# A table of due-time offsets for a planned attention and MLP kernel, replaced by another

## The chip, the cores and the metric

The kernel runs on one core of a Trainium2 chip. The metric is the device time of one execution in microseconds. Before the change it is 624.45 us, the median of three runs (622.62, 624.45 and 626.06). One further execution was taken with the hardware profiler: 630.24 us, of which 628.4 us are the span of the profile. TensorE does the matrix products, VectorE (DVE), ScalarE (ACT) and GpSimd (POOL) work on rows, and SyncE (SP) issues the transfers.

## The reference

The inputs are q, k and v of shape (4, 8, 1152, 64): 4 batches of 8 heads, 1152 positions, 64 numbers each; a weight of 512 x 1024, one of 1024 x 512 and a vector of 1024.

```python
q_pool = q.reshape(B, H, S // 2, 2, D).mean(axis=3)
scores = scale * np.matmul(q_pool, k.transpose(0, 1, 3, 2))
scores = scores - np.max(scores, axis=-1, keepdims=True)
attn = np.exp(scores)
attn = attn / (np.sum(attn, axis=-1, keepdims=True) + 1e-09)
x = np.matmul(attn, v)           # then heads side by side: 2304 rows of 512
h = x @ w_in
e = np.exp(h - np.max(h, axis=-1, keepdims=True))
solu = h * (e / (np.sum(e, axis=-1, keepdims=True) + 1e-09))
mu, var = np.mean(solu, -1, keepdims=True), solu.var(-1, keepdims=True)
ln = (solu - mu) / np.sqrt(var + 1e-06) * g_ln
out = ln @ w_out
```

So there are 32 heads of 576 queries against 1152 keys, and behind them 2304 tokens that go through two weight matrices.

## The kernel before

**Attention.** The heads are taken as 16 pairs. For a pair, keys and pooled queries are loaded, scaled and split into a coarse part and a remainder in 16 bits: the largest value qm of the queries (L683), a scale qs from it (L691, L698 and the reciprocal L703), the coarse queries qa (ACT, L823), their remainder qb (VectorE, by the helper at L473), the coarse keys (GpSimd, L722, for pair 1) and the remainder kn of the keys (VectorE, L473 again). SyncE turns qa, qb and kn by DMA transposes (L837, L733) and copies pieces on: khi (L738), w2h (L1102) and zq (L843), which holds the last 64 queries of both heads of a pair. zq reads the turned qa.

For each head TensorE first makes scores whose row maxima VectorE takes (L982, L977, L988). They are turned, shifted (L994), and put into a row of the query operand by a DMA (L1003, L1005); in the first pairs another way is used (L1011, L1021). Then TensorE makes the scores proper, a key tile of 128 at a time; ACT takes the exponential once in 32 and once in 16 bits (L1133, L1139), GpSimd forms the remainder (L1160), and TensorE multiplies with the values (vhi, vlo, from L911 and L918). VectorE divides by the sums and writes x (L1242).

**Tokens.** Each batch gives four token tiles of 128 and one half tile; SyncE merges two half tiles into one (xm, L1563). A tile is normalized, turned (xt, L1345), multiplied with w_in, goes through the exponential (L1384) and the layer norm (L1459), is turned again (lt, L1464), multiplied with w_out, copied and stored (L1539). The weights are themselves prepared from raw loads (L535) with the casts at L544 and VectorE's L554 and L560.

**What sets the order.** No step stands in the code in the order in which it runs. Each is registered with an engine, a length, a due time and what it reads and writes, and a planner orders all of them: at any moment of its own reckoning an engine takes the ready step with the smallest due time for which there is a buffer. The due time is a formula of the kernel's constants KP (L23) plus an offset from the table OFF (L24), which is looked up by the group of the step: the name of the first tile that it writes and the number of its pair, head or tile, as `kn.1` or `zq.9`.

```python
at += OFF.get(self.group((writes or reads)[0]), 0)
```

Due times also decide who gets a buffer or a bank first. After the planning each engine runs its steps in a fixed order, and waits on semaphores for what others make.

Of the kernel before, what the change touches and what calls it, by code (L numbers as in the profile page):

```python
# [42 lines left out]
class Plan:  # L43
# [50 lines left out]
    def add(self, engine, length, at, fn, reads=(), writes=(), mark=None, kind="round", also=(), calls=1, port=0):  # L94
        at += OFF.get(self.group((writes or reads)[0]), 0)
        o = Op(n=len(self.ops), engine=engine, length=length, at=at, fn=fn, mark=mark, kind=kind, calls=calls)
        o.port = port or engine == "POOL"
        reads, writes, also = ([self.place(k) for k in x] for x in (reads, writes, also))
        deps = o.deps
        for k in self._keys(reads):  # L100
            if k in self.writers:
                deps[self.writers[k]] = True
        for k in writes:
            if k in self.writers:
                deps[self.writers[k]] = True
            for r in self.readers[k]:
                deps.setdefault(r, False)
        deps.pop(o, None)
        for k in self._keys(reads):
            self.readers[k].append(o)  # L110
        for k in writes:
            self.writers[k] = o
            self.readers[k] = []
            self.parts[k[:2]][k] = 1
        for k in (*reads, *writes, *also):
            b = k[:2]
            if (b[0] in self.tags or b[0] in self.banks) and b not in o.uses:
                if b not in self.users:
                    o.new.append(b)
                o.uses.append(b)  # L120
                self.users[b] += 1
        self.ops.append(o)
# [1548 lines left out]
```

## Time and profile before

| what | value |
| --- | --- |
| median of three runs | 624.45 us |
| profiled execution | 630.24 us |
| its span | 628.4 us |
| TensorE busy | 594.5 us (95%) |
| VectorE busy | 505.1 us (80%) |
| ACT busy | 506.7 us (81%) |
| GpSimd busy | 469.0 us (75%) |
| mean granted TensorE clock | 0.98 |

The busy time counts what an engine executes, not its waits. The granted clock is the share of TensorE's full speed, 2.4 GHz, that it was given; 0.50 is 1.2 GHz, and a number between is a stretch of which a part was at either level. The chain that ended last is followed back from the last instruction, at each step to what released it; where TensorE has 71% of it, the rest is time in which TensorE waited for somebody.

### The profile page before, as it was taken

The numbers are of one execution on the slowest core, as the hardware profiler recorded it, in microseconds if no ns is written. First come the engines' busy times: TensorE is split into PE (matmuls) and PEld (weight loads), VectorE is DVE, ScalarE is ACT, GpSimd is POOL, SyncE is SP. The second block draws the span as 40 slices with busy tenths as digits, with TensorE's granted clock in tenths as the row PEclk, the third lists the DMA queues.
The fourth block names the chain that finished last, engine by engine and source line by source line (L and its number), as shares of the span: only waits on it lengthen the run. The fifth ranks groups of instructions, "written<-read, shape, count | busy, mean of one in ns | idle before, by whom it ended". The sixth has DMA issues, their size and how long they took to land.

```text
span 628.4 us, 17256 instructions
## 1 busy us (share of the span) xinstructions
PE 594.5 (95%) x6630; PEld 368.2 (59%) x6635; DVE 505.1 (80%) x1189; ACT 506.7 (81%) x978; POOL 469.0 (75%) x491
## 2 busy tenths in 40 slices
PE   8978989998888899999999999999999999999997
PEld 6747666765545465565665556556566666654453
DVE  6966788989799998878977999888989887529460
ACT  5866787998889889888998798898989989946361
POOL 5796666665777889898899889788999989932130
PEclk9996979999899899999999999999999999999999
DMA  9183967387987658767748679767697453146322
GB/s 262 35 177 98 205 179 165 75 189 154 187 225 149 133 103 182 150 151 128 142 76 144 158 142 189 139 148 111 129 164 133 81 103 79 29 67 117 69 50 68
DMA packets 183790, 83.00 MB, mean 132 GB/s; under 512 B 168604, under 2 KB 169372, under 8 KB 183708
## 3 DMA queue, kind: packets, MB, share of 16 engines
q1 hardware_dynamic: 183196, 81.18, 63.5%
q8 instruction: 52, 0.85, 0.6%
q10 hardware_dynamic: 512, 0.72, 0.3%
q14 instruction: 30, 0.25, 0.1%
HBM read 36.70 MB, written 4.72 MB: 66 GB/s over the span
## 4 chain that ended last, share of the span: by engine, by line
PE 71%; DVE 16%; ACT 4%; POOL 2%; DMA 2%; issue 2%; SPq 1%; DVEq 0%; POOLq 0%; ACTq 0%
PE bank L463 68%; DVE mx L982 6%; POOL eh L1160 2%; PE bank L1639 1%; ACT e L1139 1%; DMA zq<-q 1%; DVE wb L473 1%; DVE kn L473 1%; DVE eh L1153 1%; DVE mx L977 1%; ACT eh L1139 1%; DMA q<-c 1%; DVE ln L1459 1%; PE bank L743 1%; DVE wb L554 1%
## 5 line engine op out<-in xcount | busy, mean ns | idle before, releaser
L1160 POOL TENSOR_TENSOR eh<-e,eh 128x512 f16<-128x512 f32 (+1 forms) x278 | 331.7, 1212 | 65.2 <-ACT e L1139 24.0
L982 DVE TENSOR_REDUCE mx<-bank 128x1 f32<-128x512 f32 (+1 forms) x300 | 188.0, 653 | 25.5 <-PE bank L463 24.5
L463 PEld LDWEIGHTS <-eh 128*128 128x128 f16 x3246 | 137.9, 99 | 66.0 <-issue 9.5
L1139 ACT ACTIVATE e<-bank 128x512 f32<-128x512 f32 (+1 forms) x259 | 154.0, 614 | 24.6 <-POOL eh L1160 11.6
L1139 ACT ACTIVATE eh<-bank 128x512 f16<-128x512 f32 (+3 forms) x257 | 151.6, 616 | 27.5 <-PE bank L463 26.1
L463 PE MATMUL bank<-vhi,eh 128*128 128x65 f16 x2159 | 149.8, 196 | 7.1 <-DVE x L1242 3.0
L463 PE MATMUL bank<-q,w 128*128 128x64 f16 (+2 forms) x612 | 142.5, 294 | 6.1 <-ACT e L1139 2.2
L463 PE MATMUL bank<-q,w2h 65*128 65x512 f16 (+1 forms) x540 | 127.3, 288 | 0.0
L463 PE MATMUL bank<-w,q 128*128 128x512 f16 (+2 forms) x390 | 109.1, 339 | 4.2 <-DVE mx L982 2.6
L463 PE MATMUL bank<-wb,xt 128*128 128x512 f16 x432 | 113.0, 379 | 0.0
L463 PE MATMUL bank<-wb,lt 128*128 128x512 f16 x432 | 110.5, 379 | 0.1
L463 PE MATMUL bank<-vlo,eh 128*128 128x64 f16 x1087 | 104.5, 195 | 0.0
L463 PEld LDWEIGHTS <-w2h 65*128 65x128 f16 x540 | 45.2, 98 | 32.4 <-issue 9.3
L463 PEld LDWEIGHTS <-w 128*128 128x128 f16 x540 | 46.6, 98 | 23.9 <-issue 2.2
L463 PEld LDWEIGHTS <-lt 128*128 128x128 f16 x432 | 38.8, 98 | 37.0 <-issue 0.4
L463 PEld LDWEIGHTS <-xt 128*128 128x128 f16 x432 | 38.0, 98 | 36.5 <-issue 2.6
L1166 POOL TENSOR_TENSOR er<-r,er 128x320 f16<-128x320 f32 (+1 forms) x60 | 51.3, 857 | 8.7 <-ACT er L1150 5.0
L463 PEld LDWEIGHTS <-q 128*128 128x128 f16 x360 | 31.3, 99 | 21.1 <-issue 3.6
L1360 DVE TENSOR_REDUCE st<-bank 128x1 f32<-128x512 f32 x36 | 24.3, 682 | 21.3 <-PE bank L463 21.3
L1384 ACT ACTIVATE e<-bank,st,xs 128x512 f32<-128x512 f32 x36 | 27.7, 777 | 14.9 <-DVE st L1363 9.8
L1422 POOL TENSOR_TENSOR st<-st 128x1 f32<-128x1 f32 x18 | 4.3, 239 | 38.4 <-DVE st L1411 36.8
L1150 ACT ACTIVATE r<-bank 128x320 f32<-128x320 f32 (+1 forms) x60 | 25.6, 431 | 4.0 <-PE bank L463 3.8
(143 smaller groups left out, 900.8 us busy)
## 6 DMA issues: line engine op xcount, KB each, us to landing
vx<-in_v_dram SPq DMA_DIRECT2D x32, 288.0 KB
kt<-in_k_dram SPq DMA_DIRECT2D x31, 288.0 KB
qt<-in_q_dram SPq DMA_DIRECT2D x15, 576.0 KB
out_dram<-o SPq DMA_DIRECT2D x35, 128.0 KB
khi<-w SPq DMA_DIRECT2D x30, 144.0 KB
w2h<-w SPq DMA_DIRECT2D x30, 144.0 KB
raw<-in_moe_w_in_dram SPq DMA_DIRECT2D x8, 511.6 KB
raw<-in_moe_w_out_dram SPq DMA_DIRECT2D x8, 511.6 KB
```

What stands on the lines that cost most here:

```text
L463: nc.tensor.matmul(out=o, lhsT=a, rhs=b, start=first, stop=last, skip_group_check=True)
L473: eng.scalar_tensor_tensor(out=o, in0=a, scalar=scale, in1=b, op0=ALU.mult, op1=ALU.subtract)
L554: nc.vector.scalar_tensor_tensor(out=w32.bitcast(I32), in0=tl["raw", n][:, :, 0], scalar=5, in1=tl["wps", n].bitcast(I32), op0=ALU.logical ...
L743: nc.tensor.transpose(ps[:, c, :], tl["kt", 0][:, h, 3 * i + c, :], ident)
L977: nc.vector.tensor_reduce(out=tl["mx", g][:, 0:4, 2], in_=tl["nps", (g, m, c)], op=ALU.max, axis=AXX)
L982: nc.vector.tensor_reduce(out=tl["mx", g][:, m, c:c + 1], in_=tl["nps", (g, m, c)], op=ALU.max, axis=AXX)
L1139: nc.scalar.activation(out=o if P else o.rearrange("p (f i) -> p f i", f=2), in_=i, func=ACTF.Exp, scale=esc)
L1150: nc.scalar.activation(out=o, in_=tl[rn(u), (g, u)], func=ACTF.Exp, scale=esc)
L1160: eng.tensor_tensor(out=e[:, o:o + c.stop - c.start], in0=e32[:, c], in1=e[:, c], op=ALU.subtract)
L1166: eng.tensor_tensor(out=e[:, :, 1, :], in0=tl["r32", (g, u)][:, 0:len(RU[u]), :], in1=e[:, :, 0, :], op=ALU.subtract)
L1360: nc.vector.tensor_reduce(out=st(f), in_=tl[H_[f]], op=ALU.max, axis=AXX)
L1384: nc.scalar.activation(out=tl[E][:, f * 512:(f + 1) * 512], in_=tl[H_[f]], func=ACTF.Exp, bias=st(2), scale=xs[:, r, 3:4], accum_out=st(3 ...
```

## The change

The table OFF at L24 is replaced. Before it had 1049 entries, now it has 1058; 1042 groups are in both, and 4 of these have the same value. Nothing else in the code differs: not KP, not the planner, not a length or a buffer. The number of instructions of each kind on each engine is the same, and the steps of each engine are the same steps. In the order of 1872 planned TensorE steps, 1258 can be left where they are while the others are moved around them; on VectorE 829 of 1126, on SyncE 277 of 369.

```diff
-OFF = {'am.0': 28.38, 'am.1': -49.32, 'am.10': 1.42, 'am.11': -2.84, ...
+OFF = {'am.0': -39.66, 'am.1': -70.36, 'am.10': -7.68, 'am.11': -4.98, ...
```

The first place is on VectorE, where pair 1's keys and queries are made ready while the maxima of head 1 are taken: qm is the largest query, qs the scale, qb and kn the remainders, mx the maxima. Before:

```order
L683 TENSOR_REDUCE qm<-qt 128x1
L982 TENSOR_REDUCE mx<-bank 128x1 x2
L691 TENSOR_REDUCE qs<-bank 128x1
L698 TENSOR_SCALAR qs<-qs 128x1 x2
L982 TENSOR_REDUCE mx<-bank 128x1
L703 RECIPROCAL qs<-qs 128x1
L982 TENSOR_REDUCE mx<-bank 128x1
L1011 TENSOR_REDUCE mz<-mx 128x3
L982 TENSOR_REDUCE mx<-bank 128x1 x3
L473 SCALAR_TENSOR_TENSOR qb_85<-qt,qs,qa 128x9x64
L1021 TENSOR_SCALAR q_160<-bank 1x384
L473 SCALAR_TENSOR_TENSOR kn<-kt,qs,kn 128x18x64
```

The same place after the change:

```order
L683 TENSOR_REDUCE qm<-qt 128x1
L982 TENSOR_REDUCE mx<-bank 128x1 x2
L691 TENSOR_REDUCE qs<-bank 128x1
L698 TENSOR_SCALAR qs<-qs 128x1 x2
L982 TENSOR_REDUCE mx<-bank 128x1
L703 RECIPROCAL qs<-qs 128x1
L982 TENSOR_REDUCE mx<-bank 128x1 x2
L1011 TENSOR_REDUCE mz<-mx 128x3
L473 SCALAR_TENSOR_TENSOR qb_85<-qt,qs,qa 128x9x64
L1021 TENSOR_SCALAR q_161<-bank 1x384
L473 SCALAR_TENSOR_TENSOR kn<-kt,qs,kn 128x18x64
```

Between the reciprocal and qb stand two maxima instead of four; ahead of L683 one fewer is left too, and behind kn follow five instead of two.

The second place is on GpSimd, a little earlier: vlo is the remainder of the first pair's values, qt the pooled queries of pair 1, the COPY of L752 fills the operand w2 of head 1, and L1160 is the remainder of the exponentials. Before:

```order
L755 MEMSET w_193 1x1152
L918 TENSOR_TENSOR vlo<-vx_80,vhi_82 128x1152
L679 TENSOR_TENSOR qt<-qt 128x576
L521 MEMSET zq_86 128x128
L1160 TENSOR_TENSOR eh<-e_323,eh 128x64
```

After:

```order
L755 MEMSET w_194 1x1152
L752 COPY w_194<-w_180 64x384 x3
L918 TENSOR_TENSOR vlo<-vx_80,vhi_82 128x1152
L521 MEMSET zq_86 128x128
L679 TENSOR_TENSOR qt<-qt 128x576
```

The three copies, which stood between remainders of the exponentials some twenty rows further down, now come ahead of vlo; on ACT, L911, which vlo waits for, and the statistics L871 of the next pair have changed places.

The third place is on SyncE, where pair 9 is turned and copied on: w2h, khi and zq are operands of the score products, xm is the merged half tile, out_dram the output. Before:

```order
L651 DMA qt<-in_q_dram 128x1152
L837 DMA_TRANSPOSE q_5020<-qb_85 128x9x64 x2
L1102 DMA w2h_79<-w_4478 64x1152
L837 DMA_TRANSPOSE q_5081<-qa 128x9x64 x2
L733 DMA_TRANSPOSE w_5139<-kn 128x9x128
L843 DMA zq_86<-q_5081 64x64 x2
L1563 DMA xm<-x 64x512
L738 DMA khi<-w_5139 64x1152
```

After:

```order
L651 DMA qt<-in_q_dram 128x1152
L837 DMA_TRANSPOSE q_5027<-qb_85 128x9x64 x2
L733 DMA_TRANSPOSE w_5073<-kn 128x9x128
L837 DMA_TRANSPOSE q_5107<-qa 128x9x64 x2
L1102 DMA w2h_79<-w_4493 64x1152
L738 DMA khi<-w_5073 64x1152
L1563 DMA xm<-x 64x512
L843 DMA zq_86<-q_5107 64x64 x2
```

The copies into zq, which stood ahead of the merge xm, now stand behind it.

## Rows read from the trace of the kernel before

**Rows 1.** Head of the page: span, busy time by engine, granted clock, chain by engine

```profile
span 628.4 us, 17256 instructions
...
PE 594.5 (95%) x6630; PEld 368.2 (59%) x6635; DVE 505.1 (80%) x1189; ACT 506.7 (81%) x978; POOL 469.0 (75%) x491
...
PE 71%; DVE 16%; ACT 4%; POOL 2%; DMA 2%; issue 2%; SPq 1%; DVEq 0%; POOLq 0%; ACTq 0%
```

**Rows 2.** Busy by stretch: window, PE, PEld, DVE, ACT, POOL; PEclk, DMA share, GB/s

```profile
0.00:260.00 260.00, 234.00 (x2598) 157.92 (x2604) 220.28 (x492) 214.56 (x415) 190.57 (x200) 0.95 0.70 158
260.00:624.00 364.00, 360.48 (x4034) 210.31 (x4032) 284.78 (x699) 291.43 (x564) 278.47 (x292) 1.00 0.61 115
40.00:60.00 20.00, 15.91 (x116) 12.08 (x115) 13.66 (x29) 12.13 (x21) 14.08 (x21) 0.75 0.54 143
80.00:100.00 20.00, 18.01 (x207) 13.36 (x207) 15.37 (x36) 13.71 (x26) 9.55 (x8) 0.83 0.60 160
...
200.00:220.00 20.00, 17.14 (x158) 8.65 (x158) 19.08 (x46) 18.13 (x35) 17.05 (x18) 0.91 0.61 136
```

**Rows 3.** The same by stretches of 3 us, ahead of and behind the clock's falls

```profile
45.00:48.00 3.00, 1.66 (x18) 1.29 (x17) 2.39 (x7) 2.62 (x5) 3.00 (x4) 1.00 1.01 261
...
51.00:54.00 3.00, 3.00 (x25) 2.75 (x23) 1.67 (x4) 1.91 (x4) 1.42 (x2) 0.50 0.06 20
...
84.00:87.00 3.00, 1.44 (x6) 0.48 (x5) 2.97 (x8) 2.55 (x4) 2.75 (x3) 1.00 0.87 254
```

**Rows 4.** Timeline, TensorE: start, us, instruction, count, [idle before <- releaser]

```profile
39.62 0.59 PE L463 MATMUL bank<-w,q 128*128 128x512 f16 x2
...
49.00 0.32 PE L463 MATMUL bank<-khi,zq 128*128 128x384 f16 x1 [2.34 <-DMA zq<-q]
...
58.87 1.04 PE L463 MATMUL bank<-w,q 128*128 128x512 f16 x2
```

**Rows 5.** TensorE's waits, grouped: us in total, times, longest

```profile
PE bank L463 <- DMA zq<-q: 3.6, 2, 2.3
```

**Rows 6.** Timeline, SyncE's queue, pair 1

```profile
29.88 2.64 SPq L837 DMA_TRANSPOSE q<-qb  x2
...
42.09 1.24 SPq L843 DMA_DIRECT2D zq<-q  x2
```

**Rows 7.** Timeline, VectorE, pair 1

```profile
26.73 1.53 DVE L982 TENSOR_REDUCE mx<-bank 128x1 f32<-128x384 f32 x3
28.18 1.64 DVE L473 SCALAR_TENSOR_TENSOR qb<-qt,qs,qa 128x576 f16<-128x576 f32 x1
...
30.44 1.42 DVE L473 SCALAR_TENSOR_TENSOR kn<-kt,qs,kn 128x1152 f16<-128x1152 f32 x1
```

**Rows 8.** Timeline, GpSimd, from 19 to 43 us

```profile
19.28 2.39 POOL L918 TENSOR_TENSOR vlo<-vx,vhi 128x1152 f16<-128x1152 f32 x1 [9.02 <-ACT vhi L911]
21.63 1.42 POOL L679 TENSOR_TENSOR qt<-qt 128x576 f32<-128x576 f32 x1
...
26.24 3.21 POOL L722 TENSOR_SCALAR kn<-kt,qs 128x1152 f16<-128x1152 f32 x1
...
41.22 1.40 POOL L752 CAST w<-w 64x384 fp32r<-64x384 f32 x3
```

**Rows 9.** Timeline, the queue, VectorE and TensorE near 300 us, pair 9

```profile
298.65 1.17 SPq L843 DMA_DIRECT2D zq<-q  x2
300.54 0.46 SPq L1563 DMA_DIRECT2D xm<-x  x1
...
300.02 0.49 DVE L1242 TENSOR_TENSOR x<-bank,r 128x320 f32<-128x320 f32 x1
...
309.11 0.32 PE L463 MATMUL bank<-khi,zq 128*128 128x384 f16 x1
```

**Rows 10.** Timeline, TensorE, the last matmuls

```profile
610.28 13.54 PE L463 MATMUL bank<-wb,lt 128*128 128x512 f16 x62
```

2 lines of the change are left out of this document (1 added, 1 removed).

## The prediction

> **What bounds the kernel now.** First the head of the profile's page [rows 1]. TensorE is busy for 594.5 of 628.4 us, and 71% of the chain that ended last is its own work. So the time can only fall by the 33.9 us in which TensorE idles, and by what it loses at the lower of its two clock levels. Next the view by stretches [rows 2]: 26.0 of the 33.9 idle microseconds lie before 260 us (260.00 − 234.00), 3.5 between 260 and 624, and the rest (4.4) behind the last matmul. Behind 260 us the granted clock is 1.00 throughout, so only the first 260 us have anything to give, while anything behind them can be lost.
>
> The clock: in the stretches 40:60 and 80:100 the mean granted clock is 0.75 and 0.83 [rows 2], which is 10.0 us and 6.8 us at 1.2 GHz instead of 2.4 (twice the shortfall from 1, times 20 us). At 51:54 it reads 0.50 right behind a stretch, 45:48, in which TensorE was busy for 1.66 of 3 us; 84:87, with 1.44 of 3 us, stands ahead of the second fall [rows 3]. What half clock costs: two matmuls of 512 columns take 1.04 us at 58.87 and took 0.59 at 39.62 [rows 4], so 43% of a time at half clock is lost where TensorE has no other wait: 4.3 of the 10.0 us, 2.9 of the 6.8.
>
> The longest wait of TensorE for one result is the one at 49.00: 2.34 us for the DMA that writes zq [rows 4], 2.3 of the 3.6 us that this DMA costs in all [rows 5]. Followed back: zq is written by SyncE's queue (issues from 42.09); that queue begins pair 1 with the transposes of qb at 29.88 [rows 6], and works without a gap from there to zq; qb is written by VectorE at 28.18 for 1.64 us [rows 7], so it ends at 29.82, 0.06 us before the queue starts.
>
> **The change part by part.** Only the table OFF differs, numbers that are added to the due time of each group of steps. The set of instructions is the same on every engine; their order is not. A time in it acts only through order, so I asked of each stretch with a wait what now stands ahead of the step that is waited for.
>
> *Pair 1's keys and queries, on VectorE.* Before, four of the reductions L982 stood between the reciprocal L703 and qb; now two do. Three of them take 1.53 us [rows 7], 0.51 each, so two are 1.02 us. One more (0.51 us) leaves the row ahead of L683, with which the scales of pair 1 begin; but L683 can't start before GpSimd's copy of q, 21.63 us plus its 1.42 [rows 8], and behind L683 come a matmul and three short steps whose places are the same, so I count 0.2 of it. So qb ends 1.2 us sooner, at 28.6. The second part of kn, 30.44 on VectorE, moves with it. It ends at 31.86 now, and its transposes stand behind qb's on the queue, issued at 29.88 + 2.64 = 32.52: 0.7 us of cover, and both ends shift alike. On SyncE the same issues stand between qb and zq, two of them exchanged, so zq moves by those 1.2 us: the wait at 49.00 ends at 47.8. Lower bound 0 (GpSimd's kn, 26.24 for 3.21 us [rows 8], lies over qb and may still stretch it, or the transposes may be bound by something else), upper bound 2.34 (the wait as a whole). I take 1.2, since both ends of the chain are rows with no gap between.
>
> The reductions that went behind kn are three more than before, 1.53 us. What they hold up is the maximum of the second head, which goes into its row of q2; nothing of that is read until TensorE has passed the wait for zq, so I count 0.
>
> *GpSimd's copies for w2 (L752).* Three copies, 1.40 us, leave 41.22 and go ahead of vlo, where GpSimd idles for 9.02 us [rows 8]. From 24 to 50 us GpSimd has no gap, and TensorE waits for its rests (L1160) here and there between 41 and 45 us. So those waits end up to 1.40 us sooner; but TensorE then stands all the longer before zq. Worth 0 as long as zq is last, up to 1.4 if the queue is helped by it (no row says so); I take 0. On ACT the two casts of L544 go behind the one that writes qa, whose transposes are fourth on a queue that is busy without a gap: 0. If vlo comes so much later that the first products wait, the cover is the 9.02 us idle ahead of it, less 1.40.
>
> *From 50 to 260 us.* The work ahead of each waited-for step (the reductions L982, vhi, zq of pairs 2 to 6) is the same in both orders within a microsecond or two, with single steps traded. Bounds: at 84:87 the idle time is 1.56 us [rows 3], and I see nothing in the new order that fills it or doubles it. In 200:220 VectorE is busy for 19.08 of 20 us and ACT for 18.13, TensorE for 17.14 [rows 2]; as their work is the same, they let through a gain from the head only as far as they too start earlier. In 40:60 VectorE is busy for 13.66 of 20 us: it waits for TensorE there, so it moves with it. I count 0 for the stretch, between −1.5 and +1.5.
>
> *From 260 us on.* TensorE idles for 3.5 of 364 us, so no reordering gives much. SyncE's queue of pair 9: the load of zq now stands behind the DMA of xm, see the third rival. At the end TensorE works without a gap up to 623.82 (62 matmuls, 13.54 us from 610.28 [rows 10]), and the last copies and the store take the remaining 4.6 us in both orders: 0.
>
> Sum: −1.2 us. Of the profiled execution that is 628.4 − 1.2 = 627.2 us of span, and with the 1.8 us around it (630.24 − 628.4) 629.0 us. That execution is 0.9% above the median of the runs, 624.45 us; I put the difference on the median: 623.2 us, between 620.6 (−2.34 and −1.5) and 626 (0 and +1.5).
>
> **The rivals.**
> *First, the clock doesn't fall in the head: faster.* In 40:60 TensorE is busy for 15.91 of 20 us, of which 10 us were at half clock [rows 2]. If 1.2 us less idle time before 49 us and GpSimd's 1.4 us keep the clock at 2.4 GHz, the 4.3 us are saved too: −1.2 − 4.3 gives 618.9 us. If the fall behind 84:87 goes as well, with its 2.9 us, 616.0. For it: the two falls in the rows follow the two emptiest stretches, and little would be needed. Against it: about 1.1 us of the wait for zq stays, as does the idle time of the stretches next to it. [...]
>
> *Second, nothing gets through.* The engines behind TensorE absorb the head's gain where they are busy for 19 of 20 us: 624.4 us. For it are the rows of 200:220; against it that VectorE idles before 60 us.
>
> *Third, a wait in the part without gaps: slower.* On SyncE's queue, zq of pair 9 was issued at 298.65 and was needed at 309.11; the DMA of xm waits for x, which VectorE writes from 300.02 to 300.51, and was issued at 300.54 [rows 9]. Now zq stands behind it: issued at 301.1, 2.45 us later. For pair 1 it took from 42.09 [rows 6] to 49.00 [rows 4], 6.9 us, to be usable, with the DMA engines full (1.01 in 45:48 [rows 3]). 301.1 + 6.9 = 308.0, 1.1 us before it is needed. It decides from an x of head 15 that is over 1.1 us later, or a zq that is needed that much sooner. Then up to 2.45 us of wait, and, as behind the 1.56 us of 84:87, 6.8 us at half clock (2.9 us lost): −1.2 + 2.45 + 2.9 = +4.15, 628.6 us. Other late steps with thin cover would end about there. Against it: the DMA engines are less full there, and 1.1 us of cover are still cover.
>
> **How the numbers follow.** Forecast 0.36, first rival 0.32, second 0.12, third 0.20. The predicted time is 623.2 us; its own range is 620.6 to 626.0. To leave out no more than 2 in 10, the range goes from 616.0 (the first rival with both falls gone) to 629.0 (the third, a little more than its price). A measurement of this kernel can tell about 0.5% from no change, 3.1 us: faster is below 621.3, slower above 627.6. Faster: nearly all of the first rival (0.30) and the lower end of the others (0.07), 0.37. Slower: 0.17 of the third and 0.03 of the others, 0.20. Within: 0.43.
>
> **What would show it.** Right: the timeline of VectorE has qb's end 0.7 to 1.7 us earlier against L703's, SyncE's zq issue and TensorE's wait for it move by as much, and the granted clock still reads 0.50 behind 50 us. First rival: the same, with a clock of 1.00 in the stretch behind it. Third: a wait of TensorE for zq near 308 us, with less than 1.00 behind it. Wrong: a wait for zq that ends at 49 us or later; or a difference that lies in 100 to 260 us, where I counted nothing; or new idle time behind 260 us at another step than zq.

## The result and the profile after

The changed kernel takes 617.77 us (median of 4, 617.21 to 618.60) against 625.25 us of the kernel before: a ratio of 0.9893, 95% interval 0.9863 to 0.9923. Timed a second time, beside other kernels, it takes 617.07 against 624.32 us, 0.9877 (0.9856 to 0.9898). So it is faster by about 7 us, 1.1 to 1.2%. The forecast of 623.2 us had the sign and not the size. The number is near the 618.9 us of the first rival, and it lies in the range only because that rival stretched it; the experiments show that it came about in another way, so this was luck.

The head of the page of the changed kernel (span, busy by engine, chain by engine), for [rows 1]:

```profile
span 616.8 us, 17270 instructions
...
PE 585.2 (95%) x6635; PEld 362.1 (59%) x6635; DVE 507.0 (82%) x1189; ACT 507.7 (82%) x978; POOL 466.5 (76%) x491
...
PE 69%; DVE 18%; DMA 4%; issue 3%; ACT 2%; POOL 2%; SPq 1%; DVEq 0%; ACTq 0%; POOLq 0%
```

Of the chain that ended last TensorE has 71% before and 69% here, yet it stands still for only 5% of the span in both: the rest of the chain is not TensorE's waiting, as the part on the time before takes it.

The view by stretches of the changed kernel, for [rows 2] (window, then busy us of PE, PEld, DVE, ACT and POOL, granted clock, DMA share, GB/s):

```profile
0.00:260.00 260.00, 235.24 (x2724) 157.64 (x2725) 232.35 (x526) 223.63 (x431) 198.11 (x207) 0.99 0.73 163
260.00:612.00 352.00, 349.75 (x3913) 204.46 (x3911) 274.70 (x664) 283.41 (x547) 268.41 (x285) 1.00 0.57 114
...
40.00:60.00 20.00, 17.54 (x201) 13.42 (x202) 17.27 (x35) 15.69 (x30) 15.96 (x22) 1.00 0.65 168
80.00:100.00 20.00, 19.13 (x242) 13.21 (x241) 18.37 (x38) 17.09 (x33) 16.01 (x14) 1.00 0.73 153
200.00:220.00 20.00, 17.64 (x233) 10.69 (x232) 18.66 (x34) 18.19 (x36) 17.23 (x16) 1.00 0.46 90
```

Read against [rows 2] this looks like the first rival: the clock is 1.00 at 40:60 and at 80:100, TensorE idles as much before 260 us (24.8 us against 26.0), and the span is 11.6 us shorter. But 11.6 is more than the 7 us by which the medians differ: the profiled execution of before, 630.24 us, lies above every one of the 29 times that the kernel before had in the first set of experiments (620.63 to 627.59). It was therefore profiled again, unchanged. These are the three stretches of that second execution (f4_again), which took 624.15 us:

```profile
40.00:60.00 20.00, 17.77 (x193) 14.01 (x192) 17.14 (x34) 13.85 (x24) 17.25 (x24) 0.91 0.63 164
80.00:100.00 20.00, 18.69 (x230) 12.64 (x228) 18.38 (x39) 15.86 (x31) 15.71 (x13) 1.00 0.86 150
200.00:220.00 20.00, 17.60 (x200) 9.88 (x199) 18.18 (x34) 17.39 (x33) 15.89 (x14) 0.91 0.47 109
```

The same program, in the same order: 3.4 us at half clock in 40:60 (by the trace's records of the clock; 0.91 is rounded) where it had been 10.0, none in 80:100 where it had been 6.8. What the first 100 us lose to the clock differs from execution to execution; in both profiles of the changed kernel it is a fall of 3.4 us near 33 us. At 200:220 both executions of before read 0.91, and the changed kernel 1.00; that one goes with the order, as the next section shows.

The prediction's own place, on VectorE in the changed kernel (start, us, instruction), for [rows 7]:

```profile
26.11 1.00 DVE L982 TENSOR_REDUCE mx<-bank 128x1 f32<-128x384 f32 x2
...
27.10 2.76 DVE L473 SCALAR_TENSOR_TENSOR qb<-qt,qs,qa 128x576 f16<-128x576 f32 x1
...
30.48 1.42 DVE L473 SCALAR_TENSOR_TENSOR kn<-kt,qs,kn 128x1152 f16<-128x1152 f32 x1
```

GpSimd beside it, for [rows 8]:

```profile
21.04 1.43 POOL L679 TENSOR_TENSOR qt<-qt 128x576 f32<-128x576 f32 x1
...
26.28 3.21 POOL L722 TENSOR_SCALAR kn<-kt,qs 128x1152 f16<-128x1152 f32 x1
```

and SyncE's queue, for [rows 6 and 9]:

```profile
29.93 3.76 SPq L837 DMA_TRANSPOSE q<-qb  x2
...
42.38 1.26 SPq L843 DMA_DIRECT2D zq<-q  x2
...
289.93 0.46 SPq L1563 DMA_DIRECT2D xm<-x  x1
290.48 1.19 SPq L843 DMA_DIRECT2D zq<-q  x2
```

qb starts 1.08 us sooner than before (27.10 against 28.18) and ends at the same time (29.86 against 29.82): it takes 2.76 us instead of 1.64, until GpSimd's write of kn is over at 29.49. The queue starts where it did (29.93 against 29.88). TensorE's wait, for [rows 4], is shorter by 0.71 us all the same:

```profile
48.45 0.49 PE L463 MATMUL bank<-khi,zq 128*128 128x384 f16 x2 [1.63 <-DMA zq<-q]
```

zq is issued 0.29 us later than before and is there 0.55 us sooner, so the time from issue to use was 0.84 us less; and in the new order four score products now stand ahead of the wait instead of behind it.

### The profile page after: what moved, and what is told of

Read it like the earlier page. It is cut to its first block, busy times and chain, and to the rows that moved or that the text cites. A ratio compares the mean times of both kernels' runs of the same rounds, so it can differ in the third digit from the quotient of the medians.

```text
span 616.8 us, 17270 instructions
## 1 busy us (share of the span) xinstructions
PE 585.2 (95%) x6635; PEld 362.1 (59%) x6635; DVE 507.0 (82%) x1189; ACT 507.7 (82%) x978; POOL 466.5 (76%) x491
## 4 chain that ended last, share of the span: by engine, by line
PE 69%; DVE 18%; DMA 4%; issue 3%; ACT 2%; POOL 2%; SPq 1%; DVEq 0%; ACTq 0%; POOLq 0%
PE bank L463 68%; DVE mx L982 6%; DMA raw<-in_moe_w_out_dram 2%; POOL eh L1160 1%; DVE mx L1040 1%; DMA zq<-q 1%; DVE kn L473 1%; DVE ln L1459 1%; DVE wm L560 1%; DVE wb L473 1%; ACT e L1139 1%; DVE eh L1153 1%; DMA xt<-xn 1%; DVE mx L977 1%; DVE x L1242 1%
## 5 line engine op out<-in xcount | busy, mean ns | idle before, releaser
L1160 POOL TENSOR_TENSOR eh<-e,eh 128x512 f16<-128x512 f32 (+1 forms) x278 | 323.1, 1178 | 57.4 <-ACT e L1139 28.5
L982 DVE TENSOR_REDUCE mx<-bank 128x1 f32<-128x512 f32 (+1 forms) x300 | 187.0, 653 | 17.1 <-PE bank L463 16.2
L463 PEld LDWEIGHTS <-eh 128*128 128x128 f16 x3246 | 133.4, 98 | 60.9 <-issue 7.1
L463 PE MATMUL bank<-vhi,eh 128*128 128x65 f16 x2159 | 145.2, 194 | 5.6 <-DVE x L1242 2.3
L463 PE MATMUL bank<-q,w2h 65*128 65x64 f16 (+1 forms) x540 | 126.4, 287 | 0.0
L463 PE MATMUL bank<-w,q 128*128 128x512 f16 (+2 forms) x390 | 106.8, 333 | 4.2 <-DVE mx L982 3.4
L463 PE MATMUL bank<-wb,lt 128*128 128x512 f16 x432 | 107.9, 379 | 0.4 <-DVE e L1391 0.4
L463 PE MATMUL bank<-vlo,eh 128*128 128x64 f16 x1087 | 102.5, 194 | 0.0
L463 PEld LDWEIGHTS <-xt 128*128 128x128 f16 x432 | 38.2, 98 | 35.6 <-issue 0.7
L1166 POOL TENSOR_TENSOR er<-r,er 128x320 f16<-128x320 f32 (+1 forms) x60 | 52.6, 879 | 2.4 <-DVE mx L982 0.7
L1422 POOL TENSOR_TENSOR st<-st 128x1 f32<-128x1 f32 x18 | 5.7, 315 | 42.1 <-DVE st L1411 42.1
L1391 DVE SCALAR_TENSOR_TENSOR e<-bank,st,e 128x512 f32<-128x512 f32 x36 | 26.4, 744 | 2.0 <-ACT e L1384 1.2
```

The lines of the kernel that those rows point to most:

```text
L463: nc.tensor.matmul(out=o, lhsT=a, rhs=b, start=first, stop=last, skip_group_check=True)
L982: nc.vector.tensor_reduce(out=tl["mx", g][:, m, c:c + 1], in_=tl["nps", (g, m, c)], op=ALU.max, axis=AXX)
L1160: eng.tensor_tensor(out=e[:, o:o + c.stop - c.start], in0=e32[:, c], in1=e[:, c], op=ALU.subtract)
L1166: eng.tensor_tensor(out=e[:, :, 1, :], in0=tl["r32", (g, u)][:, 0:len(RU[u]), :], in1=e[:, :, 0, :], op=ALU.subtract)
L1391: nc.vector.scalar_tensor_tensor(out=tl[E][:, s], in0=tl[H_[f]], scalar=st(1), in1=tl[E][:, s], op0=ALU.mult, op1=ALU.mult, accum_out=st(5 ...
```

## The experiments

Each kernel was timed beside the kernel before; the ratios are to that, with 95% intervals. Several of them join the two orders. There the due times are no longer a formula plus an offset, but a list with the place that each step had in one or the other kernel's plan, and the planner takes no step before its time:

```diff
-        at += OFF.get(self.group((writes or reads)[0]), 0)
+        at = AT[len(self.ops)]
...
+            o.ok_at = max(0, o.at)
...
-            limit = 1e9 if not todo else now_mark + (self.window if todo < len(marks) else FIRST)
+            limit = t
```

The traces show that the joined kernels are what they are meant to be: ahead of the joint VectorE, ACT and GpSimd run in the one order, and from some 25 us behind it in the other, with at most ten of their some 2400 steps elsewhere, all behind 220 us.

**Is it the head's wait and the clock behind it?** First the wait at 49 us was filled, in the old order:

```diff
             if m == 4 and P:
+                if (g, c) == (2, 0):
+                    for _ in range(12):
+                        mm(ps, flat(tl["q1", P][:, h])[:, 0:128], tl["w1", g][:, 0:PW], True, True)
```

> The kernel before, with its old table, and 12 further matmuls of 384 columns ahead of the first product that waits for zq of pair 1; their product is overwritten. At some 0.16 us each they lie inside the 2.34 us in which TensorE waited there. Theory 1 (the clock): the time was lost because TensorE's clock fell behind that wait; with TensorE busy in it the granted clock stays at 1.00 from 50 to 60 us and the time falls by 4 to 5.5 us, to about 620. Theory 2 (the order): the time is gained by waits that the new order shortens all along the first 260 us; then work that nobody needs changes nothing or costs up to 1 us, about 625.

Measured: 625.12 us, ratio 1.0011 (0.9992 to 1.0029): nothing. The fill did its work: TensorE stood still for 0.16 us ahead of the product that waits for zq, instead of 2.34 [rows 4].

```profile
48.59 0.32 PE L463 MATMUL bank<-khi,zq 128*128 128x384 f16 x1 [0.16 <-issue]
```

But the clock had its falls elsewhere in this execution, most at 20:40, ahead of the fill, where the program is that of before, so one profile doesn't show what the fill did to the clock; the time of twelve runs shows that it gained nothing:

```profile
20.00:40.00 20.00, 17.79 (x165) 14.45 (x165) 15.89 (x34) 15.48 (x40) 19.74 (x20) 0.80 0.38 63
40.00:60.00 20.00, 19.48 (x211) 14.68 (x209) 16.86 (x34) 13.72 (x23) 16.71 (x22) 0.94 0.61 159
80.00:100.00 20.00, 17.43 (x195) 12.03 (x195) 17.24 (x35) 14.43 (x28) 11.56 (x10) 0.91 0.86 156
```

Then the wait was made longer, in the new order, by three loads into tiles that nobody reads:

```diff
         def q_half():
+            if P == 1:
+                for t in gz:
+                    nc.sync.dma_start(out=t, in_=g_ln.rearrange("(i p) -> p i", p=128))
```

> The changed kernel, with three small loads that nobody reads issued on SyncE's queue ahead of the two copies into zq of pair 1, so that zq comes some 1.9 us later and TensorE waits about 3.5 us instead of 1.63. Theory 1 (the clock): the clock falls to 1.2 GHz behind the wait, as in the kernel before, and the time grows by 1.9 + 4 to 5 us, to about 624. Theory 2 (the order): it grows by 1.9 us or less, to 619.7 at most, since the order is that of the changed kernel everywhere.

Measured: 621.82 us, ratio 0.9971 (0.9949 to 0.9993), 4 to 4.8 us more than the changed kernel by the medians. The delay was larger than meant; SyncE's queue and TensorE's wait in this kernel:

```profile
42.06 4.87 SPq L845 DMA_DIRECT2D gz<-in_moe_g_ln_dram  x3
46.98 1.23 SPq L847 DMA_DIRECT2D zq<-q  x2
...
49.43 0.65 PE L463 MATMUL bank<-khi,zq 128*128 128x384 f16 x2 [3.10 <-DMA zq<-q]
```

zq is issued 4.6 us later, TensorE's wait for it is 3.10 us and ends at 49.43 (48.45 in the changed kernel, 47.25 in its second profile), and the clock is at 0.91 in 40:60. The twelve runs fall into two groups: seven with a mean clock of 0.992 to 0.993 took 620.2 to 622.4 us, five with 0.979 to 0.985 took 623.9 to 625.6. The profile is of the first group. So a wait that is at least 1.5 us longer here costs some 3 us in some executions and 6 to 7, at a lower clock, in others: theory 1's 624 us is the second group, and theory 2's 619.7 was not reached. That doesn't show that the old order paid this price, and e1_fill says that it did not.

Next the two orders were joined at 48 us, once each way.

> The order of the changed kernel for the first 48 us, and that of the kernel before for all the rest (each step's due time is set to its place in the one or the other). Theory 1: the head's part of the gain is one fall of the clock, 4.3 to 5.5 us, so about 620; the falls behind 84 and 160 us stay. Theory 2: the head gives only what its waits give, 0.5 us at 49 us, so about 624.7; the gain is in the rest.

Measured: 623.93 us, 0.9989 (0.9974 to 1.0005), near theory 2's 624.7 and far from theory 1's 620. The new head alone can't be told from nothing. It is the part on which the whole forecast rested.

> The converse: the order of the kernel before for the first 48 us, that of the changed kernel for the rest. Theory 1: the first fall of the clock stays, the later ones go as far as the new order fills their waits: 1 to 3 us faster than before, about 622.5 to 624. Theory 2: nearly the whole gain, 618.3.

Measured: 619.74 us, 0.9921 (0.9898 to 0.9944): about two thirds of the gain with the old head (by the interval, half to nearly all), less than theory 2's 618.3 and more than theory 1 allowed. The profile of this kernel has 13.7 us at half clock ahead of 60 us, more than the 10.2 of the first profile of before, and its span, 618.3 us, is 10.1 us shorter than there and 4.1 us shorter than in the second:

```profile
20.00:40.00 20.00, 17.77 (x163) 14.45 (x164) 16.02 (x35) 15.49 (x40) 19.63 (x19) 0.81 0.34 61
40.00:60.00 20.00, 17.62 (x168) 13.70 (x166) 15.43 (x32) 12.72 (x22) 14.81 (x21) 0.85 0.57 149
```

Theory 1 in its first form falls. What the head is worth stays loose: 0.7 us put in alone, 1.7 to 2.7 us by its lack here (by the ratios).

**Where behind 48 us?** The new order up to a place, the old one behind it:

> The new order up to 100 us of the plan, the old one behind it; 48 us gave 623.9, 150 us 620.3. Theory 2 with the gain spread evenly: 622. If the waits at 84 to 88 us of the kernel before (1.9 us, and the fall of the clock behind them) are what was gained between 48 and 150 us: 620.5.

> The new order up to 150 us of the plan, the old order behind it. Theory 1b: the falls near 160 and 214 us stay, since the order around them is the old one; the gain is that of the first 100 us only, 1 to 2.5 us, so 622 to 623. Theory 2: the shorter waits lie behind, so 0.5 to 1 us, about 623.5.

> The new order up to 205 us of the plan, the old order behind it. Theory 1b: all falls of the clock behind 60 us are gone; what is left of the gain behind is 0.5 to 1 us, so about 618.5. Theory 2: the waits behind 230 us (252.59, 332.58, 343.30, 370.06 and 404.25 in the profile before, 3.3 us together, against 1.7 of the like after) are back: 2 to 2.8 us slower than the changed kernel, about 620.2.

| new order up to | median | ratio, 95% interval |
| --- | --- | --- |
| 48 us | 623.93 | 0.9989 (0.9974 to 1.0005) |
| 100 us | 622.96 | 0.9971 (0.9943 to 0.9998) |
| 150 us | 620.26 | 0.9937 (0.9916 to 0.9959) |
| 205 us | 620.85 | 0.9940 (0.9921 to 0.9958) |
| the end (two timings) | 617.77, 617.07 | 0.9893, 0.9877 |

The ratios are the safer comparison, since the kernels were timed in three sets. By them 3.2 us are gained between 48 and 150 (3.7 by the medians; 1.1 of it up to 100 us and 2.1 behind, a division that is not clear of the noise), nothing that shows between 150 and 205, and 2.9 to 3.9 behind 205, each of the two gains within about 1.8 us (an estimate from the intervals). "New to 100", at 622.96, fits a gain that is spread out and not the 620.5 of the waits at 84 to 88 us. "New to 150" gained more than either theory gave (622 to 623.5). "New to 205" comes out near theory 2's 620.2; the condition of theory 1b for 618.5, no fall behind 60 us, was not met, as is seen below. The profiles say about the same stage by stage. The stages are set by VectorE's reciprocal at the end of a head (the 2nd, 6th, 9th, 12th, 14th, 21st and 27th) and by TensorE's last matmul; in brackets TensorE's idle time:

| ends with head | before, again | new to 48 | new to 150 | new to 205 | changed, again |
| --- | --- | --- | --- | --- | --- |
| 2 | 67.1 (9.1) | 66.9 (8.4) | 66.2 (7.9) | 66.2 (8.1) | 65.0 (7.5) |
| 6 | 55.8 (3.6) | 55.9 (3.8) | 54.5 (2.8) | 54.0 (2.4) | 54.6 (2.9) |
| 9 | 51.9 (5.7) | 52.8 (6.4) | 51.3 (5.3) | 51.8 (5.5) | 52.1 (5.8) |
| 12 | 51.4 (5.6) | 50.8 (5.2) | 51.1 (5.4) | 51.3 (6.0) | 49.9 (6.4) |
| 14 | 38.2 (1.1) | 38.2 (1.1) | 38.2 (1.1) | 37.7 (1.1) | 36.7 (0.4) |
| 21 | 115.8 (2.3) | 115.4 (1.9) | 115.7 (2.4) | 115.5 (2.0) | 116.3 (2.3) |
| 27 | 100.2 (1.0) | 100.1 (0.6) | 100.2 (0.6) | 100.2 (1.0) | 99.4 (0.0) |
| last matmul | 137.2 (0.0) | 137.4 (0.3) | 137.2 (0.0) | 137.2 (0.0) | 136.9 (0.0) |

One cell up to head 9 is not much evidence by itself: between the two profiles of the changed kernel those stages differ by up to 1.2 us. But the sums hold over all profiles without a fill near 150 us. The stages of heads 6 and 9 together take 105.8 to 107.5 us in the seven profiles with the new order from 48 to 150 us, and 107.7 to 110.3 in the five others. From head 9 to the last matmul it is 438.5 to 439.2 us in the five with the new order behind 205 us, and 441.8 to 443.0 in the seven with the old one.

Behind 205 us (the stages of heads 12 to the last) the changed kernel is 2.7 us shorter than "new to 205": 1.4 in the stage of head 12, 1.0 in that of head 14, 0.8 in that of head 27, 0.3 in the last, less 0.8 lost (head 21). In the stage of head 12 its idle time is even longer, 6.4 against 6.0 us. What differs there is the clock. The same place in "new to 205" and, 1.7 us later, in the changed kernel:

```profile
200.00:204.00 4.00, 2.65 (x13) 0.98 (x13) 3.97 (x6) 3.77 (x8) 1.54 (x2) 1.00 0.69 142
204.00:208.00 4.00, 3.57 (x28) 2.02 (x27) 3.97 (x11) 3.21 (x7) 4.00 (x4) 0.61 0.01 2
```

```profile
201.00:205.00 4.00, 2.66 (x18) 1.09 (x17) 3.97 (x7) 3.78 (x8) 1.93 (x2) 1.00 0.69 146
205.00:209.00 4.00, 2.98 (x29) 1.42 (x29) 3.97 (x10) 3.77 (x8) 3.48 (x4) 1.00 0.01 2
```

Up to there TensorE was as little busy in the one as in the other (2.65 and 2.66 of 4 us); then the one runs at half clock for 3.1 us and the other at full. The fall stands here in all seven profiles of kernels with the old order behind 205 us and no fill there, and in none of the five that have the new one. What in the order decides it, these runs don't show.

Behind it are waits. TensorE's waits of 0.5 us and more between 230 and 420 us in the kernel before, profiled again:

```profile
246.43 0.38 PE L463 MATMUL bank<-q,w 128*128 128x512 f16 x1 [0.74 <-ACT e L1139]
...
326.44 0.38 PE L463 MATMUL bank<-q,w 128*128 128x512 f16 x1 [0.58 <-ACT e L1139]
...
337.15 0.38 PE L463 MATMUL bank<-w,q 128*128 128x512 f16 x1 [0.51 <-DVE qs L691]
...
363.94 0.19 PE L463 MATMUL bank<-vhi,eh 128*128 128x65 f16 x1 [0.53 <-DVE x L1242]
...
398.15 0.38 PE L463 MATMUL bank<-w,q 128*128 128x512 f16 x1 [0.95 <-DVE c L994]
```

Four of the five, all but that for x, stand in "new to 205" too, a little earlier. In the changed kernel the largest there are these:

```profile
310.91 0.19 PE L463 MATMUL bank<-vhi,eh 128*128 128x65 f16 x1 [0.46 <-DVE x L1242]
...
333.42 0.38 PE L463 MATMUL bank<-w,q 128*128 128x512 f16 x1 [0.47 <-DVE qs L691]
334.52 0.20 PE L463 MATMUL bank<-vhi,eh 128*128 128x65 f16 x1 [0.42 <-DVE qs L698]
```

The waits for the exponential and for the shifted maxima (L994) are gone, 2.3 us together; all waits behind the 12th head sum to 4.0 us in the one and to 2.2 in the other (2.6 in its second profile).

**What are the falls near 160 and 214 us worth?** Two kernels in the old order had matmuls laid into TensorE's idle time there. In the first the fills took time in the plan, and with that the order behind 205 us changed as well; the second mends this.

```diff
+                if e == "PE" and (141e3 < t < 152e3 or 194e3 < t < 203e3) and t > self.filled + 150:
...
+                        extra.append((t, lambda i=i: self.fill(i)))
```

> The order of the kernel before, with 57 pairs of small matmuls (128 columns, their product is never read) put where its plan has TensorE idle near 141 to 152 and 194 to 203 us. In all three profiles with the old order behind 48 us the clock fell near 160 and near 214 us (6.6 us at half clock between 120 and 230), in none of the three with the new one. Theory 1b (the rest's gain is those falls): they are gone, and the time falls by 2 to 3 us, to about 622. Theory 2 (shorter waits, most of all behind 230 us): no change, 624.2, or up to 1 us more.

Measured: 625.04 us, 1.0007 (0.9988 to 1.0027). The clock is 1.00 from 120 to 230 us and the 12th head ends 2.7 us sooner than in the kernel before profiled again, but the stages behind, whose order had changed from about 211 us on, are longer by 2.3 us. It settles nothing.

> The order of the kernel before in every step, with 99 matmuls of 128 columns (their product is never read) between its steps where its plan has TensorE idle near 141 to 152 and 194 to 203 us. This mends the fill run before, in which the order behind 205 us had changed too. Theory 1b (the falls of the clock near 160 and 214 us are what the old order loses there): the clock is 1.00 from 120 to 230 us and the time falls by 1.5 to 3 us, to 621.5 to 623. Theory 2 (waits, and falls cost little where other engines are waited for anyway): within 1 us of the kernel before, whatever the clock.

Measured: 622.96 us, 0.9977 (0.9959 to 0.9994), 1.4 us faster. The stretches of this kernel:

```profile
140.00:160.00 20.00, 19.68 (x296) 14.35 (x295) 18.13 (x37) 17.07 (x34) 15.05 (x15) 1.00 0.87 169
160.00:180.00 20.00, 18.72 (x201) 10.38 (x200) 19.67 (x42) 18.59 (x35) 16.35 (x16) 1.00 0.88 239
200.00:220.00 20.00, 18.23 (x256) 11.77 (x253) 18.77 (x36) 18.18 (x35) 16.98 (x15) 1.00 0.56 113
```

The clock stays up, and that is worth 1.4 us, between 0.4 and 2.6: about a fifth of the gain, at the edge of the 1.5 to 3 of theory 1b and above the 0 to 1 of theory 2, with an interval that reaches into both.

The runs on record bear on the whole of the clock's part. The mean granted clock is kept for 89 runs of the kernel before; 29 of them had 0.992 to 0.997, the range of all nine runs of the changed kernel. These 29 took 624.2 us in the median (621.5 to 625.3), the nine 617.2 (615.5 to 618.6). So at the same mean clock nearly the whole difference is still there, 7.0 us: the clock was not what the change was worth. The mean doesn't say where in a run a fall stood.

**Two controls and the step that failed.**

> The kernel before, unchanged, profiled once more. If the falls of the clock in the first 100 us belong to the order, they stand again at 50 and 88 us and cost 10 and 6.8 us at half clock; if they belong to the single execution, they stand elsewhere (20 to 40 us) or are shorter, and the falls near 160 and 214 us are there again.

Those of the first 100 us belong to the single execution: 624.61 us, 1.0005 (0.9983 to 1.0027), and a profile with a fall of 3.4 us at 42, none at 88 us, none near 160, which was expected again, and 3.4 us at 209. Even the wait of the forecast isn't there: the first product with zq waits 0.74 us, for a step of VectorE.

```profile
48.32 0.32 PE L463 MATMUL bank<-khi,zq 128*128 128x384 f16 x1 [0.74 <-DVE r L1231]
```

> The changed kernel itself, once more. Both theories: 617.5 to 618.5 us with a mean clock of 0.99 or more. Should its median be near 620, the new order up to 150 us carried all of the gain.

617.07 us, 0.4 below what was expected, with a clock of 0.992 to 0.997.

Last, the coarse keys of pair 1 were taken from GpSimd and given to ACT in the changed order (its list of due times held, KH emptied):

```diff
-'KH': [1]
+'KH': []
```

> The changed kernel with one step on another engine: the coarse keys of pair 1 are written by ACT instead of GpSimd, so that VectorE writes qb of pair 1 without GpSimd beside it. If qb took 2.76 us because GpSimd's write of kn ran beside it, it takes 0.7 to 0.9 us now, ends some 1.5 to 2 us sooner, and the wait for zq of pair 1 (1.63 us) shrinks by 1 us or more or goes. If it took 2.76 us for another reason, it stays. The time: 0 to 1.5 us less, since the steps behind it on ACT start 1.2 us later.

Measured: 616.03 us, 0.9870 (0.9848 to 0.9892). VectorE and TensorE in this kernel:

```profile
26.88 1.25 DVE L474 SCALAR_TENSOR_TENSOR qb<-qt,qs,qa 128x576 f16<-128x576 f32 x1
```

```profile
46.14 0.48 PE L464 MATMUL bank<-khi,zq 128*128 128x384 f16 x2 [0.41 <-DVE r L1232]
```

qb takes 1.25 us instead of 2.76 and the wait for zq is gone: GpSimd's write was what stretched it. 1.25 is above the 0.7 to 0.9 expected; GpSimd's copy of qa lies beside it for 0.64 us, but that this is the reason isn't shown (for a later pair, at 368.47, the copy lies beside qb for 0.74 us and qb takes 0.80). This kernel's median is the lowest of all, 1.0 us below the changed kernel's in the same set, but the times of the two overlap (615.63 to 617.81, and 615.54 to 617.23), so it isn't shown to be faster than that.

## Why the prediction was right or wrong

**qb 1.2 us sooner: wrong.** The start moved as worked out, 1.08 us; the duration did not hold. I took 1.64 us from [rows 7] as the step's own, though GpSimd's kn lay over it there too [rows 8]. It ends 0.37 to 0.38 us behind GpSimd's kn in both kernels, and in every one of the thirteen profiles that have this write, so starting it sooner gave it only more of the overlap. The lower bound, 0, was the right value, and the prediction named this reason there; g3_act shows the cause.

**The wait at 49.00: wrongly taken for the order's.** TensorE waits 2.34 us for zq in one execution of before and not at all in the other; in the two of the changed kernel it is 1.63 us and nothing. Filling it gave nothing. A term of the sum stood on one execution's row.

**First rival, the clock in the head: its number came, its mechanism did not.** The falls at 50 and 88 us were the profiled execution's. The Trainium skill, TensorE: Matmul & The Clock Gate, Part 1 (What's actually happening), says of the slow matmuls at a kernel's start that their number varies from run to run of the same kernel. The two profiles of before show it for falls in the middle of a kernel too: up to the last matmul they have 23.9 and 6.8 us at half clock. With 17.1 us more of it the first span is 6.1 us longer, nearly all of it ahead of the 6th head's end. The price of 43% was too high for a whole run: ten runs of the kernel before with a mean clock of 0.975 to 0.983 took 626.5 us in the median, 2.3 more than the 29 with 0.992 to 0.997, for some 15 us more at half clock (an estimate from the mean clocks), which is 0.16 us for each.

**"From 50 to 260 us 0, between −1.5 and +1.5": wrong.** The largest error, and by the prediction's own signs one that shows it wrong, since part of the difference lies behind 100 us. From 48 to 150 us the new order is worth 3.2 to 3.7 us. In the stages of heads 2, 6 and 9 no single wait explains it: the idle time is lower by 0.5, 1.0 and 1.1 us (new to 150 against new to 48), and the 3.4 us at half clock near 160 in the one are absent in the other (but they are absent in before profiled again as well). I had asked of each large wait what stands ahead of it, found the same work, and left out the many waits of 0.3 to 0.8 us. That it is these which became shorter is read from single profiles and not shown by an experiment. I also gave no price to the fall that [rows 2] has in 200:220 (0.91), the one that goes with the order.

**"From 260 on no reordering gives much": half wrong.** The idle time there was only 3.5 us, but a third of it went (2.2 and 2.3 us in the two profiles of the changed kernel); I had these rows and counted 0. With the fall near 214 us, the order behind 205 us is worth 2.9 to 3.9 us.

**Second rival: wrong.** What was gained early reached the end: the stage behind the 27th head is 137 us long in all kernels.

**Third rival: did not happen.** The queue did what was worked out, zq behind xm, but the product with zq of pair 9 comes at 298.78 at the earliest, 8.3 us after the first issue, and waits for nothing:

```profile
298.78 0.32 PE L463 MATMUL bank<-khi,zq 128*128 128x384 f16 x1
```

**The end: right.** From the 27th head to the last matmul 137.2 us before, 136.9 after, and 4.6 us behind it in both.

**What stays open:** what in the order keeps the clock up near 205 us; which waits the gain between 48 and 150 us consists of; and some 2.6 us by which TensorE is busy for less in the changed kernel (585.2) than in before profiled again (589.3), when 3.4 us less at half clock are taken off at 43%. A matmul of 65 columns is drawn with 0.19 us though the next may start 0.03 us later, so waits of up to 0.16 us would count as busy; that this is where they are is argued, not shown.

## What to carry to other kernels

Profile the kernel before twice before a term is built on one wait or one fall of the clock: here the wait was gone in the next execution, and of the two falls of the clock one was gone and one a third as long. When a whole order is exchanged, join the two orders at a few places and time each, rather than look for the one step: here two stretches gained 3 to 4 us each, the predicted head next to nothing, and the clock was perhaps a fifth. Compare runs at the same mean clock before the clock is taken for the cause. And take a step's duration as its own only after a look at who runs beside it.

## What the runs showed of the hardware

VectorE's remainder of 128x576 took 1.25, 1.64 or 2.76 us, as GpSimd's write of 128x1152 (3.21 us) lay beside it for 0, 1.3 or 2.4 us, and ended 0.37 to 0.38 us behind that write in all thirteen profiles that have it. Three loads of a vector of 1024 in single elements held SyncE's queue for 4.87 us, 1.6 each, where a copy into zq takes 0.6. The granted clock of one program was at half speed for 23.9 us in one execution and for 6.8 in another. One fall of it, near 205 to 214 us, stood in seven of seven profiles with one order of the steps and in none of five with another.
